# A prologue in another order: mask copies on ScalarE, GpSimd's splits and constants rearranged, set-up work moved behind a later unit

## The chip, the cores and the metric

The kernel runs as one program on one core of a Trainium2 chip. The metric is the device time in microseconds, from the start of the program to the end of its last instruction; a run is timed several times and its median is compared. The core has five engines that work beside each other, each through its own list of instructions in order: TensorE (PE in the profile, its weight loads PEld), VectorE (DVE), ScalarE (ACT), GpSimd (POOL) and SyncE (SP, which here only issues DMA transfers). They wait for each other by semaphores.

## The reference

Attention over clusters, then a mixture of experts on its output. The batch is 4, with 8 heads, 768 positions and head dimension 64.

```
q_assign = argmax(q_n . c_n), k_assign = argmax(k_n . c_n)       # 16 centroids for each head
scores   = where(q_assign == k_assign, q k^T / 8, -1e9)
attn     = softmax(scores);  out = attn v
x        = out as (3072 tokens, 512)
g_idx    = argmax(x w_group), e_idx = argmax(x w_expert[g_idx])  # 4 groups of 4 experts
y        = softmax weights of both choices * (relu(x w1) w2)     # of the chosen expert alone
```

## The kernel before

The 32 heads (4 batches of 8) are worked on in pairs: pair p holds heads 2p and 2p + 1, one in partitions 0 to 63 and one in 64 to 127. For each pair the kernel loads k, q and v (`load`, `loadv`), splits each into a 16-bit part and a 16-bit rest, the "hi" and the "lo" part (`split`, `splitv`: ScalarE writes hi; lo comes from VectorE, or in the prologue for pairs 0 and 1 partly from GpSimd), computes the clusters (`assign`: 36 small matmuls, then maxima and comparisons on VectorE that give a one-hot row), and copies the parts by DMA into the tiles `A` (hi parts and mask rows) and `B` (`spread`).

A head is then 9 coarse and 9 fine units of 512 columns. A coarse unit (`coarse`) is one product on TensorE and one maximum over it on VectorE (`tensor_reduce`, "reduce" below); after the ninth, `rowmax` turns the 9 maxima into one row for each query. A fine unit (`fine`) multiplies again with the mask and the row maximum in the contraction, ScalarE takes the exp (`p32`), GpSimd the rest of it (`pl`, the line with `op=ALU.subtract` in `fine`), and 5 units later (`LAG`) TensorE multiplies it with v (`av`, "P·V" below, 16 matmuls). Coarse units run 13 units ahead of the fine ones at first and up to 18 later. `pp` holds 7 buffers of `p32` and `pl`.

The masks of heads 0 to 3 are made by `mask_now`: six transposes for q and six for k, each followed by a copy of 16 rows into `A`, by ScalarE for q and by VectorE for k. The row maximum of heads 0 and 1 is made in `rowmax`'s first branch: a last maximum on VectorE (`m7`, 6 columns from 18), a small ScalarE copy into `st`, six transposes on TensorE, and a ScalarE copy into `A`.

The prologue, up to the loop over fine units, is written out by hand: constants (32 rows of each of the 16 halves of the eight `A` tiles, and two columns of each of the four `V` tiles, set by GpSimd), the centroids, pair 0, coarse units of head 0, the splits of pair 1 on GpSimd, four coarse units of head 1, the clusters and masks of pair 1, and the load of pair 2. Then `R.setup` and `cfg["setup"]` make what the router and the experts need later: the router's weights `WR` (two VectorE instructions after the load of `wf`), `ones`, `low`, `cb` and others, lists of slots by some fifty small GpSimd instructions, and seven DMA transfers (`wf`, `zrow`, five of `table`). In the loop `at(g, f)` runs f beside fine unit g.

A scheduler of the compiler's front end decides how the instructions of one engine stand in its list, within the dependences and within the edges that `tc.issue_after(x)` adds: whatever the block traces on x's engine stands behind x there.

Of the kernel before, what the change touches and what calls it, by code (L numbers as in the profile page):

```python
# [14 lines left out]
F32 = mybir.dt.float32  # L15
I32 = mybir.dt.int32
AF = mybir.ActivationFunctionType
ALU = mybir.AluOpType
AX = mybir.AxisListType
# [6 lines left out]
SQ = 16.0  # L26
# [10 lines left out]
def attention(ctx, tc, qT, kT, vr, cen, R, DEN, cfg):  # L37
# [16 lines left out]
    EARLY = ()  # L54
    GAP, RM, RL = 1, 2, 9
    EVEN = 16
    DVE_LO = [()] * 8
    WHOLE16 = 2, 3, 4
    DVE_END = (0, 2, 4, 6, 8), (0, 1, 2, 3, 7, 8)
# [21 lines left out]
    def load(p):  # L81
        b, pr = p // NP, p % NP
        kx = ld.tile([P, S], F32, name="kx")
        qx = ld.tile([P, S], F32, name="qx")
        nc.sync.dma_start(out=kx, in_=kT[b, pr])
        nc.sync.dma_start(out=qx, in_=qT[b, pr])
        st[p] = [qx, kx]
# [61 lines left out]
    def pairs(x):  # L149

        h = struct.pack("<e", x)
        return struct.unpack("<f", h + h)[0]

    for i in range(8):
        nc.gpsimd.memset(QA[i].bitcast(F32)[64:96], pairs(PSHIFT))
        nc.gpsimd.memset(KA[i].bitcast(F32)[64:96], pairs(SQ * SQ))
    for i in range(4):
        nc.gpsimd.memset(V[i][:, :, :, 128:130], SQ)

# [20 lines left out]
    def split(p, w, pool=False):  # L180
        x = st[p][w]
        if (p, "s") not in st:

            st[p, "s"] = sp.tile([P, 4, S], F16, name="parts")
        hi, lo = (st[p, "s"][:, i] for i in ((0, 2), (3, 1))[w])
        with bound():
            nc.scalar.activation(out=hi, in_=x, func=AF.Copy, scale=SQ)
        lo_part(lo, x, hi, pool)
        st[p, w] = (hi, lo)
# [40 lines left out]
    def splitv(p, pool=False):  # L230
        x = st[p][2]
        vt = V[p % 4]
        with bound():
            nc.scalar.activation(out=vt[:, :, :, 64:128], in_=x, func=AF.Copy, scale=SQ)
        lo_part(vt[:, :, :, 0:64], x, vt[:, :, :, 64:128], pool)
# [50 lines left out]
                nc.sync.dma_start(out=KA[h % 8][64:64 + C], in_=mk[64 + C * i:64 + C * i + C])  # L286
            ready.add(h)

    def mask_now(h, pool):

        for t, dst in ((0, QA[h]), (1, KA[h])):
            tp = pool[0].tile([P, 512], F32, name=pool[1]).bitcast(F16)
            for c in range(NCH):
                nc.tensor.transpose(out=tp[0:OZ, c * P:(c + 1) * P], in_=ozs[h // 2][:, t, h % 2, c], identity=ident)
            if t == 0:
                nc.scalar.activation(out=dst[64:64 + C], in_=tp[64:64 + C, :S], func=AF.Copy, scale=-32768.0)
            else:
                nc.vector.tensor_scalar(out=dst[64:64 + C], in0=tp[64:64 + C, :S], scalar1=-32768.0, scalar2=32768.0, op0=ALU.mult, op1=ALU.add)

# [10 lines left out]
    def coarse(h, u, pool=(ps_c, "psc")):  # L310

        assert h < 4 or h in ready
        j, i = u // 3, u % 3
        if u == 0:
            cparts[h] = MP[h % 3]
        mp = cparts[h][:, j]
        pc = pool[0].tile([P, 512], F32, name=pool[1])
        off = 0
        for (c, k0, k1) in segs(u, S):
            last["mm"] = nc.tensor.matmul(out=pc[:, off:off + k1 - k0], lhsT=QA[h % 8][0:80, c * P:(c + 1) * P], rhs=KA[h % 8][0:80, k0:k1], start=True, stop=True)  # L320
            off += k1 - k0
        n = 1 + i % 2
        nc.vector.tensor_reduce(out=(mp[:, 0, 0:1], mp[:, :, 1], mp[:, 1, 0:1])[i], in_=pc.rearrange("p (a x) -> p a x", a=n), axis=AX.X, op=ALU.max)  # L323
        if u == 8 and h > 1:
            if h < 5:
                nc.gpsimd.memset(MH[h % 3][:, NCH:P], 0.0)
            nc.vector.tensor_reduce(out=pc[:, 0:NCH], in_=cparts.pop(h).rearrange("p j a x -> p (j a) x"), axis=AX.X, op=ALU.max)
            nc.vector.tensor_scalar(out=MH[h % 3][:, 0:NCH], in0=pc[:, 0:NCH], scalar1=-1.0 / (SQ * SQ), scalar2=None, op0=ALU.mult)
# [92 lines left out]
    def at(g, f, *a):  # L421
        jobs.setdefault(int(g), []).append((f, a))
# [63 lines left out]
    banks = itertools.cycle(((ps_c, "psc"), (ps_f, "psf")))  # L486
    for u in range(9):
        coarse(0, u, next(banks))
    mask_now(1, (ps_o, "pso"))
    spread(0, (1,), part=(1,))  # L490
    run(rowmax(0))

    splitv(0, True)
    split(1, 1, True)
    split(1, 0, True)
    splitv(1, True)
    with tc.issue_after(last["mm"].ins), tc.issue_after(last["max"].ins):
        for u in range(AHEAD0 - 9):
            coarse(1, u, next(banks))
        run(assign(1))  # L500
        spread(1)
        mask_now(2, (ps_m, "psm"))
        mask_now(3, (ps_m, "psm"))
    load(2)
    loadv(2)
    at(0, split, 2, 0)
    at(1, split, 2, 1)
    R.setup()
    cfg["setup"]()
    prev = []  # L510

    def av_next(g):
# [40 lines left out]
class Router:  # L553
# [9 lines left out]
    def setup(self):  # L563
        nc, const, N, E, BS, KD = self.nc, self.const, self.N, self.E, self.BS, self.KD
        wf = const.tile([P, KD, 20], F32, name="wf")
        nc.sync.dma_start(out=wf, in_=self.wr)
        self.WR = const.tile([P, 2, KD, 20], F16, name="WR")
        nc.vector.tensor_scalar(out=self.WR[:, 0], in0=wf, scalar1=WRS, scalar2=None, op0=ALU.mult)
        nc.vector.scalar_tensor_tensor(out=self.WR[:, 1], in0=wf, scalar=WRS, in1=self.WR[:, 0], op0=ALU.mult, op1=ALU.subtract)
        self.ones = const.tile([P, P], F16, name="ones")  # L570
        nc.vector.memset(self.ones, 1.0)
        self.low = const.tile([P, P], F16, name="low")
        nc.gpsimd.affine_select(out=self.low, in_=self.ones, pattern=[[1, P]], compare_op=ALU.is_gt, fill=0.0, base=0, channel_multiplier=-1)
        self.desc = const.tile([P, 30, 4], F32, name="desc4")
        nc.gpsimd.iota(self.desc, [[0, 30], [-1, 4]], base=4, channel_multiplier=0, allow_small_or_imprecise_dtypes=True)
        self.ebase = const.tile([P, E], F32, name="ebase")
        nc.gpsimd.iota(self.ebase, [[BS, E]], base=0, channel_multiplier=0, allow_small_or_imprecise_dtypes=True)
        self.cb = const.tile([P, E], F32, name="cb")
        NT = N // P
        self.pay = const.tile([P, NT, 2], F32, name="pay")  # L580
        nc.gpsimd.iota(self.pay[:, :, 0], [[P, NT]], base=0, channel_multiplier=1, allow_small_or_imprecise_dtypes=True)
        zrow = const.tile([P, 2 * KD], F16, name="zrow")
        nc.vector.memset(zrow, 0.0)
        nc.sync.dma_start(out=self.xbuf[N:N + 1].rearrange("o (p x) -> (o p) x", p=P), in_=zrow)
        em = self.em = const.tile([P, (E + 1) * BS // P // 5, 2], F32, name="em")
        nc.vector.memset(em[:, :, 0:1], float(N))
        nc.vector.memset(em[:, :, 1:2], 0.0)
        self.lg, self.last, self.sent, self.apart, self.done = {}, {}, [], True, -1

        self.reset()  # L590
# [1123 lines left out]
```

## Time and profile before

| | us |
|---|---|
| time, median of 3 runs | 705.99 |
| lowest, highest run | 704.86, 707.33 |
| the profiled execution's own time | 705.2 |
| its span, first to last instruction | 703.4 |
| TensorE busy in the span | 676.3 (96%) |
| VectorE busy | 580.7 (83%) |
| ScalarE busy | 501.8 (71%) |
| GpSimd busy | 461.3 (66%) |

The change touches the first 60 us or so of the span. In the page's strip of 40 slices (17.6 us each) TensorE is busy five tenths in the first slice, eight in the second and third and nine or more from the fourth on. All times of rows below count from the start of the span. A busy time of TensorE is modelled and matmuls overlap, so its idle time reads as a lower bound.

### The profile page before, as it was taken

What the parts mean: (1) busy time and instruction counts of PE and PEld (TensorE: products, weight loads), DVE (VectorE), ACT (ScalarE), POOL (GpSimd) and SP (SyncE); (2) the same over time, 40 slices, a digit from 0 to 9 for tenths busy, and PEclk for the clock granted to TensorE, in tenths of its full rate; (3) what the DMA queues carried; (4) which work ended last, traced back from release to release, by engine and by line L of the source; (5) the groups of instructions that cost most, each with busy time, mean ns of one, the idle gap of its engine ahead of it and who ended that gap; (6) DMA issues with size and microseconds to landing.
All of it is one profiled execution on the core that took longest, in us unless ns stands there. A gap on an engine that the chain in (4) does not pass through costs nothing.

```text
span 703.4 us, 25950 instructions
## 1 busy us (share of the span) xinstructions
PE 676.3 (96%) x10528; PEld 582.3 (83%) x10528; DVE 580.7 (83%) x1226; ACT 501.8 (71%) x948; POOL 461.3 (66%) x522
## 2 busy tenths in 40 slices
PE   5889999999999999999999999999999999999995
PEld 3677888888878888887878867898799999999995
DVE  5998988899888998989888766868688788888861
ACT  5558898898897988878897346664655666766742
POOL 9768888899998999989995044335534254443542
PEclk9999999999999999999999999999999999999998
DMA  8865736647566375641765089889989789888711
GB/s 254 204 183 150 202 102 170 157 111 210 105 160 166 92 208 108 134 119 31 175 140 108 25 307 334 306 323 245 347 233 323 243 306 292 299 295 289 215 65 36
DMA packets 89527, 136.74 MB, mean 194 GB/s; under 512 B 41507, under 2 KB 59427, under 8 KB 89384
## 3 DMA queue, kind: packets, MB, share of 16 engines
q1 hardware_dynamic: 83884, 121.32, 61.1%
q0 software_dynamic: 5344, 13.38, 5.7%
q8 instruction: 102, 1.67, 1.0%
q14 instruction: 41, 0.34, 0.2%
q10 hardware_dynamic: 156, 0.03, 0.0%
HBM read 93.17 MB, written 13.99 MB: 152 GB/s over the span
## 4 chain that ended last, share of the span: by engine, by line
PE 71%; DVE 13%; ACT 9%; issue 4%; DMA 2%; POOL 1%; POOLq 0%; DVEq 0%; SPq 0%; ACTq 0%
PE psh L1065 17%; PE psy L1099 14%; PE pso L395 11%; PE psf L362 6%; PE psc L320 6%; PE psf L363 6%; DVE mpart L323 5%; PE psy L1123 4%; ACT p L367 3%; PE psm L1151 2%; PE psm L253 2%; ACT ph L371 1%; PE psm L1033 1%; PE psm L633 1%; ACT psm L853 1%
## 5 line engine op out<-in xcount | busy, mean ns | idle before, releaser
L374 POOL TENSOR_TENSOR pl<-p 128x512 f16<-128x512 f32 x193 | 198.6, 1055 | 19.7 <-ACT p L367 18.5
L323 DVE TENSOR_REDUCE mpart<-psc 128x1 f32<-128x512 f32 (+1 forms) x282 | 188.4, 680 | 18.4 <-PE psc L320 16.5
L367 ACT ACTIVATE p<-psf 128x512 f32<-128x512 f32 x288 | 172.0, 599 | 40.2 <-PE psf L363 37.0
L395 PE MATMUL pso<-V,pl 128*128 128x65 f16 (+1 forms) x1968 | 161.1, 193 | 0.0
L362 PE MATMUL psf<-A 82*128 82x384 f16 (+2 forms) x576 | 143.9, 275 | 2.1 <-ACT p L367 0.8
L363 PE MATMUL psf<-B 128*128 128x384 f16 (+2 forms) x576 | 143.7, 274 | 0.0
L395 PEld LDWEIGHTS <-pl 128*128 128x128 f16 x1968 | 130.8, 97 | 1.8 <-issue 0.4
L395 PEld LDWEIGHTS <-p 128*128 128x128 bf16 x1632 | 112.4, 98 | 20.4 <-issue 0.5
L395 PE MATMUL pso<-V,p 128*128 128x65 f16 x1632 | 120.8, 193 | 0.0
L374 POOL TENSOR_TENSOR pl<-p,ph 128x512 f16<-128x512 f32 x84 | 96.8, 1160 | 22.6 <-POOL pl L374 8.3
L320 PE MATMUL psc<-A 80*128 80x512 f16 (+1 forms) x376 | 107.0, 328 | 4.8 <-DVE mpart L323 3.4
L1070 ACT ACTIVATE hh<-psh 128x256 f16<-128x256 f32 (+14 forms) x136 | 45.8, 347 | 74.2 <-PE psh L1065 72.6
L1023 POOL DMA_INDIRECT xg<-xbuf,ri x32 | 37.8, 1180 | 75.5 <-PE psm L1033 30.2
L1071 DVE SCALAR_TENSOR_TENSOR hl<-psh,hh 128x256 f16<-128x256 f32 (+14 forms) x136 | 47.0, 366 | 33.0 <-ACT hh L1070 32.3
L363 PEld LDWEIGHTS <-B 128*128 128x128 f16 x576 | 56.8, 99 | 13.1 <-issue 4.0
L1065 PE MATMUL psh<-xT,wh0a 128*128 128x272 f16 (+14 forms) x512 | 65.9, 246 | 1.7 <-DMA st<-w 1.0
L362 PEld LDWEIGHTS <-A 82*128 82x128 f16 x576 | 56.0, 98 | 10.2 <-issue 1.5
L1065 PE MATMUL psh<-xT,wl0a 128*128 128x272 f16 (+7 forms) x256 | 59.4, 245 | 0.0
L1065 PE MATMUL psh<-xT,wh0b 128*128 128x272 f16 (+6 forms) x448 | 57.1, 245 | 0.1
L371 ACT CAST ph<-p 128x512 f16<-128x512 f32 x84 | 51.9, 618 | 2.3
L1065 PE MATMUL psh<-xT,wl0b 128*128 128x240 f16 (+6 forms) x224 | 52.3, 244 | 0.0
L320 PEld LDWEIGHTS <-A 80*128 80x128 f16 x384 | 37.4, 99 | 15.9 <-issue 6.3
(330 smaller groups left out, 1600.6 us busy)
## 6 DMA issues: line engine op xcount, KB each, us to landing
st<-w SPq DMA_DIRECT2D x88, 512.0 KB
B<-parts SPq DMA_DIRECT2D x64, 192.0 KB
wh<-w SPq DMA_DIRECT2D x21, 512.0 KB
wl<-w SPq DMA_DIRECT2D x19, 512.0 KB
kx<-kT SPq DMA_DIRECT2D x16, 384.0 KB
qx<-qT SPq DMA_DIRECT2D x16, 384.0 KB
vx<-vr SPq DMA_DIRECT2D x16, 384.0 KB
A<-parts SPq DMA_DIRECT2D x32, 192.0 KB
```

The source lines that it names most:

```text
L320: last["mm"] = nc.tensor.matmul(out=pc[:, off:off + k1 - k0], lhsT=QA[h % 8][0:80, c * P:(c + 1) * P], rhs=KA[h % 8][0:80, k0:k1], start=T ...
L323: nc.vector.tensor_reduce(out=(mp[:, 0, 0:1], mp[:, :, 1], mp[:, 1, 0:1])[i], in_=pc.rearrange("p (a x) -> p a x", a=n), axis=AX.X, op=ALU ...
L362: nc.tensor.matmul(out=o, lhsT=KA[h % 8][0:82, ks], rhs=QA[h % 8][0:82, q0:q1], start=True, stop=False)
L363: nc.tensor.matmul(out=o, lhsT=KBs[h][:, ks], rhs=QBs[h][:, q0:q1], start=False, stop=True)
L367: cfg["exp"] = nc.scalar.activation(out=p32, in_=pf, func=AF.Exp, scale=QK / (SQ * SQ))
L371: nc.scalar.copy(out=ph, in_=p32)
L374: lo = (nc.vector if u in (EARLY if h < 2 else DVE_LO[h % 8] if h < NH - 2 else DVE_END[h - NH]) else nc.gpsimd).tensor_tensor(out=pl, in0 ...
L395: nc.tensor.matmul(out=O[:, col:col + v.shape[-1]], lhsT=p[:, bs], rhs=v, start=c == 0 and q == 0 and i == 0, stop=c == NCH - 1 and i == l ...
L1065: self.mm = nc.tensor.matmul(out=ph[:, 0:n], lhsT=w[:, k, f * P:(f + 1) * P], rhs=xT[:, a, k, 0:n], start=i == 0, stop=i == 3 * KD - 1)
L1070: nc.scalar.activation(out=hh[:, f], in_=ph[:, 0:M], func=AF.Relu)
L1071: self.ev = nc.vector.scalar_tensor_tensor(out=hl[:, f], in0=ph[:, 0:M], scalar=0.0, in1=hh[:, f], op0=ALU.max, op1=ALU.subtract)
L1099: self.mm = nc.tensor.matmul(out=py[:, 0:n], lhsT=w[:, f, d * P:(d + 1) * P], rhs=a[:, f, 0:n], start=i == 0, stop=i == len(prods) - 1)
```

## The change

Six edits, all in `attention`:

- `mask_now(1, ...)` gets `both=True`: the mask copy of k for head 1 is a ScalarE activation, with scale and bias from `mscale` and `mbias`, where a VectorE `tensor_scalar` stood.
- GpSimd sets the constants of `A` tiles 0 and 1 only at the start; those of tiles 2 to 7 come behind the splits of pair 1.
- The splits of pair 1 come in the order k, q, v of pair 0, v of pair 1, where v of pair 0 came first.
- `load(2)` is written ahead of the coarse units of head 1 and of the clusters and masks of pair 1.
- The splits of pair 2 get an edge behind the maximum that `rowmax` made last on VectorE when they run (`last["max"]`, head 0's).
- `R.setup` and `cfg["setup"]` run beside fine unit 6 (`SETUP = 6`), behind the latest reduce on VectorE and the latest `pl` on GpSimd, where they stood ahead of the loop.

```diff
--- before.py
+++ after.py
@@ -54,6 +54,7 @@
     EARLY = ()
     GAP, RM, RL = 1, 2, 9
     EVEN = 16
+    SETUP = 6
     DVE_LO = [()] * 8
     WHOLE16 = 2, 3, 4
     DVE_END = (0, 2, 4, 6, 8), (0, 1, 2, 3, 7, 8)
@@ -151,9 +152,12 @@
         h = struct.pack("<e", x)
         return struct.unpack("<f", h + h)[0]
 
-    for i in range(8):
-        nc.gpsimd.memset(QA[i].bitcast(F32)[64:96], pairs(PSHIFT))
-        nc.gpsimd.memset(KA[i].bitcast(F32)[64:96], pairs(SQ * SQ))
+    def constants(heads):
+        for i in heads:
+            nc.gpsimd.memset(QA[i].bitcast(F32)[64:96], pairs(PSHIFT))
+            nc.gpsimd.memset(KA[i].bitcast(F32)[64:96], pairs(SQ * SQ))
+
+    constants(range(2))
     for i in range(4):
         nc.gpsimd.memset(V[i][:, :, :, 128:130], SQ)
 
@@ -286,7 +290,7 @@
                 nc.sync.dma_start(out=KA[h % 8][64:64 + C], in_=mk[64 + C * i:64 + C * i + C])
             ready.add(h)
 
-    def mask_now(h, pool):
+    def mask_now(h, pool, both=False):
 
         for t, dst in ((0, QA[h]), (1, KA[h])):
             tp = pool[0].tile([P, 512], F32, name=pool[1]).bitcast(F16)
@@ -294,6 +298,8 @@
                 nc.tensor.transpose(out=tp[0:OZ, c * P:(c + 1) * P], in_=ozs[h // 2][:, t, h % 2, c], identity=ident)
             if t == 0:
                 nc.scalar.activation(out=dst[64:64 + C], in_=tp[64:64 + C, :S], func=AF.Copy, scale=-32768.0)
+            elif both:
+                nc.scalar.activation(out=dst[64:64 + C], in_=tp[64:64 + C, :S], func=AF.Identity, scale=mscale[64:64 + C], bias=mbias[64:64 + C])
             else:
                 nc.vector.tensor_scalar(out=dst[64:64 + C], in0=tp[64:64 + C, :S], scalar1=-32768.0, scalar2=32768.0, op0=ALU.mult, op1=ALU.add)
 
@@ -320,7 +326,7 @@
             last["mm"] = nc.tensor.matmul(out=pc[:, off:off + k1 - k0], lhsT=QA[h % 8][0:80, c * P:(c + 1) * P], rhs=KA[h % 8][0:80, k0:k1], start=True, stop=True)
             off += k1 - k0
         n = 1 + i % 2
-        nc.vector.tensor_reduce(out=(mp[:, 0, 0:1], mp[:, :, 1], mp[:, 1, 0:1])[i], in_=pc.rearrange("p (a x) -> p a x", a=n), axis=AX.X, op=ALU.max)
+        last["red"] = nc.vector.tensor_reduce(out=(mp[:, 0, 0:1], mp[:, :, 1], mp[:, 1, 0:1])[i], in_=pc.rearrange("p (a x) -> p a x", a=n), axis=AX.X, op=ALU.max)
         if u == 8 and h > 1:
             if h < 5:
                 nc.gpsimd.memset(MH[h % 3][:, NCH:P], 0.0)
@@ -486,14 +492,16 @@
     banks = itertools.cycle(((ps_c, "psc"), (ps_f, "psf")))
     for u in range(9):
         coarse(0, u, next(banks))
-    mask_now(1, (ps_o, "pso"))
+    mask_now(1, (ps_o, "pso"), True)
     spread(0, (1,), part=(1,))
     run(rowmax(0))
 
-    splitv(0, True)
     split(1, 1, True)
     split(1, 0, True)
+    splitv(0, True)
     splitv(1, True)
+    load(2)
+    constants(range(2, 8))
     with tc.issue_after(last["mm"].ins), tc.issue_after(last["max"].ins):
         for u in range(AHEAD0 - 9):
             coarse(1, u, next(banks))
@@ -501,12 +509,20 @@
         spread(1)
         mask_now(2, (ps_m, "psm"))
         mask_now(3, (ps_m, "psm"))
-    load(2)
     loadv(2)
-    at(0, split, 2, 0)
-    at(1, split, 2, 1)
-    R.setup()
-    cfg["setup"]()
+
+    def behind_max(w):
+        with tc.issue_after(last["max"].ins):
+            split(2, w)
+
+    at(0, behind_max, 0)
+    at(1, behind_max, 1)
+    def setup():
+        with tc.issue_after(last["red"].ins), tc.issue_after(cfg["lo"].ins):
+            R.setup()
+            cfg["setup"]()
+
+    at(SETUP, setup)
     prev = []
 
     def av_next(g):
```

What the edits do to the lists of three engines is shown next. The line numbers of the changed program are higher than those of the kernel before, by 4 in `mask_now`, by 6 in `coarse`, `rowmax` and `fine`, and by 16 in the router and the experts; `p_...` are exps by buffer, `A_165` to `A_168` the A tiles of heads 0 to 3.

VectorE around the last maximum of head 1 (`m_742` before, `m_656` after); `mpart_200` are reduces of head 2. Before:

```order
L323 TENSOR_REDUCE mpart_200<-psc 128x2
L260 TENSOR_TENSOR psm<-psm,mx 128x384
L334 TENSOR_REDUCE m_742<-mpart_199 128x6
L323 TENSOR_REDUCE mpart_200<-psc 128x1
L261 TENSOR_TENSOR psm<-psm,desc 128x384
L199 SCALAR_TENSOR_TENSOR parts<-kx,parts 128x768
L263 TENSOR_REDUCE mw<-psm 128x24
L323 TENSOR_REDUCE mpart_200<-psc 128x1
L265 TENSOR_TENSOR oh<-psm,mw 128x6x32 x2
```

In the changed program:

```order
L340 TENSOR_REDUCE m_656<-mpart_199 128x6
L329 TENSOR_REDUCE mpart_200<-psc 128x1
L265 TENSOR_TENSOR psm<-psm,desc 128x384
L203 SCALAR_TENSOR_TENSOR parts<-kx,parts 128x768
L267 TENSOR_REDUCE mw<-psm 128x24
L584 TENSOR_SCALAR WR<-wf 128x80
L269 TENSOR_TENSOR oh<-psm,mw 128x6x32 x2
L585 SCALAR_TENSOR_TENSOR WR<-wf,WR 128x80
L587 MEMSET ones 128x128
L599 MEMSET zrow 128x4
L602 MEMSET em 128x85
L603 MEMSET em 128x85
```

`WR`, the memsets and, one row further down, `cb` now stand behind the maximum of head 1 and ahead of the fourth reduce of head 2; before, `WR` and `cb` stood ahead of that maximum and the memsets at the very start.

ScalarE from the exp of fine unit 3 to that of unit 6; `parts<-kx` and `parts<-qx` are hi parts of a pair, `A_167` and `A_168` the mask copies of q for heads 2 and 3, `st<-m_...` the copy of head 1's maximum. Before:

```order
L367 ACTIVATE p_632<-psf 128x512
L367 ACTIVATE p_691<-psf 128x512
L296 ACTIVATE A_167<-psm 16x768
L367 ACTIVATE p_717<-psf 128x512
L296 ACTIVATE A_168<-psm 16x768
L187 ACTIVATE parts<-kx 128x768
L187 ACTIVATE parts<-qx 128x768
L234 ACTIVATE V_176<-vx 128x12x64
L335 ACTIVATE st<-m_742 128x6
L339 ACTIVATE A_166<-psf,obias,oscale 18x768
L367 ACTIVATE p_758<-psf 128x512
```

In the changed program:

```order
L373 ACTIVATE p_546<-psf 128x512
L373 ACTIVATE p_605<-psf 128x512
L238 ACTIVATE V_175<-vx 128x12x64
L373 ACTIVATE p_631<-psf 128x512
L191 ACTIVATE parts<-kx 128x768
L300 ACTIVATE A_167<-psm 16x768
L191 ACTIVATE parts<-qx 128x768
L300 ACTIVATE A_168<-psm 16x768
L238 ACTIVATE V_176<-vx 128x12x64
L341 ACTIVATE st<-m_656 128x6
L345 ACTIVATE A_166<-psf,obias,oscale 18x768
L373 ACTIVATE p_672<-psf 128x512
```

The hi parts of k and q of pair 3 stood behind both mask copies and now stand ahead of the first and the second; all six first exps now stand ahead of the mask copies.

GpSimd around the set-up; `pl<-p_584` before is the pl of fine unit 0, `pl<-p_672` and `pl<-p_788` after are those of units 6 and 7. Before:

```order
L197 TENSOR_TENSOR V_174<-vx,V_174 128x12x64
L573 AFFINE_SELECT low<-ones 128x128
L575 IOTA desc_502 128x120
L577 IOTA ebase 128x16
L581 IOTA pay 128x24
L785 IOTA io 128x16
L792 MEMSET capr 1x1 x13
L792 MEMSET capr 1x2
L792 MEMSET capr 1x1
L796 MEMSET capn 1x1 x16
L799 MEMSET four 1x1 x16
L803 IOTA io_573 128x288
```

In the changed program:

```order
L380 TENSOR_TENSOR pl<-p_672 128x512
L591 IOTA desc_706 128x120
L593 IOTA ebase 128x16
L597 IOTA pay 128x24
L801 IOTA io 128x16
L808 MEMSET capr 1x1 x13
L808 MEMSET capr 1x2
L808 MEMSET capr 1x1
L812 MEMSET capn 1x1 x16
L815 MEMSET four 1x1 x16
L819 IOTA io_777 128x288
L821 MEMSET svals 128x36
```

The block from the iota of `desc` to the memset of `svals` stood behind the split of v, ahead of all pl; it now stands behind the pl of unit 6, and the pl of unit 7 follows it. `low` and two iotas come behind that one.

## Rows read from the trace of the kernel before

**Rows 1.** Stretches of the span: length, busy us of each engine, granted clock, DMA

```profile
20.60:23.90 3.30, 1.90 (x17) 1.08 (x15) 3.21 (x7) 1.21 (x2) 3.30 (x56) 0.98 0.89 231
23.90:27.10 3.20, 3.20 (x16) 1.83 (x14) 2.80 (x7) 1.72 (x3) 1.70 (x7) 0.50 1.05 270
...
34.00:38.40 4.40, 3.16 (x56) 2.13 (x55) 4.40 (x9) 1.90 (x3) 0.00 (x0) 1.00 0.92 205
...
44.00:54.00 10.00, 10.00 (x188) 8.07 (x187) 9.77 (x21) 5.63 (x10) 9.93 (x9) 1.00 0.61 181
...
64.00:110.00 46.00, 45.58 (x866) 37.39 (x863) 41.09 (x91) 40.57 (x79) 39.74 (x38) 1.00 0.60 154
```

**Rows 2.** TensorE's waits from 38 to 110 us: total, times, longest

```profile
PE psf L338 <- ACT st L335: 0.4, 1, 0.4
```

**Rows 3.** Timeline of VectorE, 20 to 46 us: start, us, instruction, idle before

```profile
21.01 0.56 DVE L298 TENSOR_SCALAR A<-pso 16x768 f16<-16x768 f16 x1
21.59 0.17 DVE L334 TENSOR_REDUCE m<-mpart 128x6 f32<-128x18 f32 x1
...
25.57 0.16 DVE L594 COPY cb<-ebase 128x16 f32<-128x16 f32 x1
...
28.28 0.57 DVE L568 TENSOR_SCALAR WR<-wf 128x80 f16<-128x80 f32 x1
...
29.30 0.58 DVE L569 SCALAR_TENSOR_TENSOR WR<-wf,WR 128x80 f16<-128x80 f32 x1
...
31.10 1.50 DVE L199 SCALAR_TENSOR_TENSOR parts<-kx,parts 128x768 f16<-128x768 f32 x1
...
38.00 0.16 DVE L334 TENSOR_REDUCE m<-mpart 128x6 f32<-128x18 f32 x1
...
44.63 0.99 DVE L199 SCALAR_TENSOR_TENSOR V<-vx,V 128x768 f16<-128x768 f32 x1
```

**Rows 4.** Part 5 of the page, the reduces: busy us, mean ns, idle before

```profile
L323 DVE TENSOR_REDUCE mpart<-psc 128x1 f32<-128x512 f32 (+1 forms) x282 | 188.4, 680 | 18.4 <-PE psc L320 16.5
```

**Rows 5.** Timeline of ScalarE, 18 to 33 us

```profile
18.87 0.84 ACT L187 ACTIVATE parts<-kx 128x768 f16<-128x768 f32 x1 [1.01 <-DMA kx<-kT]
...
25.97 0.84 ACT L187 ACTIVATE parts<-qx 128x768 f16<-128x768 f32 x1
...
30.18 0.80 ACT L296 ACTIVATE A<-psm 16x768 f16<-16x768 f16 x1 [0.69 <-PE psm L294]
...
31.63 0.80 ACT L296 ACTIVATE A<-psm 16x768 f16<-16x768 f16 x1
```

**Rows 6.** Timeline of TensorE, first matmul of pair 2's clusters

```profile
32.48 0.18 PE L253 MATMUL psm<-CH,parts 128*128 128x32 f16 x1 [0.23 <-ACT A L296]
```

**Rows 7.** Chain that ended last, matmuls of pair 0's clusters: start, us, count

```profile
8.57 1.11 PE psf L253 x35
```

**Rows 8.** Timeline of GpSimd, 21 to 52 us, single instructions

```profile
21.01 0.29 POOL L573 TENSOR_SCALAR_AFFINE_SELECT low<-ones 128x128 f16<-128x128 f16 x1
21.27 0.38 POOL L575 IOTA desc<- 128x120 f32 x1
...
23.82 0.12 POOL L805 MEMSET svals<- 128x36 bf16 x1
...
24.14 0.15 POOL L807 IOTA svals<- 128x6 bf16 x1
...
40.78 1.04 POOL L374 TENSOR_TENSOR pl<-p 128x512 f16<-128x512 f32 x1 [7.28 <-ACT p L367]
...
44.77 1.76 POOL L374 TENSOR_TENSOR pl<-p 128x512 f16<-128x512 f32 x1
...
50.20 1.03 POOL L374 TENSOR_TENSOR pl<-p 128x512 f16<-128x512 f32 x1
```

**Rows 9.** Timeline of TensorE, first P·V of fine units 10 and 14

```profile
48.17 0.19 PE L395 MATMUL pso<-V,p 128*128 128x65 f16 x1
...
52.75 0.22 PE L395 MATMUL pso<-V,p 128*128 128x65 f16 x2
```

## The prediction

> **What bounds the kernel now.** I read the stretches of the span first. Behind 64 us TensorE is busy 45.58 of 46 us, and it stays so; from 44 to 54 us it is busy all the time [rows 1]. A change in the prologue can therefore give back only what TensorE loses before about 40 us: 1.40 of the 3.30 us from 20.6 to 23.9, 1.24 of the 4.40 from 34 to 38.4, and the stretch from 23.9 to 27.1, where the granted clock was 0.50 (the 1.2 GHz level) [rows 1]. Second view, TensorE's waits: from 38 us on it waits 0.4 us for ScalarE's copy that starts the row maximum of head 1 [rows 2]. That one ends a longer starvation. TensorE takes its list in order, and the six transposes of that row maximum stand ahead of every fine unit from unit 6 on. They wait for VectorE's last maximum of head 1, at 38.00 [rows 3]. So the first question is how much sooner than 38.00 that maximum comes. After it TensorE is full, and the second question is what the change puts in its way there. Third view, the engines' own lists, for both questions.
>
> **Part 1: what leaves VectorE and ScalarE's turn before 38.00.** VectorE loses the mask copy of k, head 1 (0.56 at 21.01), the copy of cb (0.16) and two WR instructions (0.57, 0.58): 1.87 us by their rows [rows 3]. In addition the lo part of k, pair two, took 1.50 there where a like one takes 0.99 (44.63) [rows 3]: if it is alone next time, 0.5 more. Upper bound of the gain: 2.4 us.
> But VectorE is not alone in that chain. The order shows that ScalarE now makes the copies of k and q of pair three ahead of the mask copy of q, head 3, where both stood behind it. Before, that copy ended at 31.63 + 0.80 = 32.43 [rows 5], and the next assignment's 36 matmuls started right behind it, at 32.48, waiting for it [rows 6]. After: minus 0.58, since the maximum of head 0 comes at once behind the ninth reduce (21.59 against 21.01 [rows 3]); plus 0.84, since two copies of 0.84 come in front of it and one, q of pair two, leaves (25.97) [rows 5]; minus at most 0.69, ScalarE's wait ahead of 30.18 that may be filled [rows 5]. It ends between 32.0 and 32.7. Behind it come the assignment (1.11 for 35 matmuls [rows 7]), one coarse unit with its hand-over (about 0.6, an estimate from the reduce of 0.68 [rows 4]) and four VectorE instructions, two reduces of 0.68 and two of about 0.57: 4.2 us, against 5.57 from 32.43 to 38.00. The maximum then comes at 36.2 to 36.9, 1.1 to 1.8 sooner. Lower bound 0.7: in TensorE's new list the P·V of units 2 and 3 stands ahead of the masks of head 3 and waits for GpSimd's pl, one of which took 1.76 where others take 1.03 [rows 8]. I take **1.4 us sooner**, ScalarE's path, not VectorE's sum.
>
> **Part 2: what is put behind it.** The router's and the experts' setup moves behind fine unit 6. On GpSimd it ran from 21.01 to 24.14 + 0.15 = 24.29, less about 0.15 for one memset of another part: 3.1 us [rows 8], when GpSimd had nothing urgent. Now 2.67 of it (21.27 to 23.94) stand between the pl of unit 6 and that of unit 7, the rest one unit later. GpSimd is idle 7.28 us ahead of unit 6 [rows 8], but the setup stands behind unit 6, so that idle time does not take it. From 44 to 54 GpSimd is busy 9.93 of 10 us [rows 1]; its pl queue is dense and P·V in TensorE's list waits for it. How late may pl be? For unit 10 it ends at 44.77 + 1.76 = 46.53 and P·V starts at 48.17; for unit 14 at 51.23 against 52.75 [rows 8, 9]. The slack is 1.64 and 1.52. A queue 3.1 later eats it and holds TensorE 3.1 - 1.52 = **1.6 us**. Bounds: zero, if TensorE is late there for another reason; 2.2, below.
> VectorE gets the two WR and cb (1.31 by their rows [rows 3]) and four small memsets behind the maximum of head 1, ahead of the fourth reduce of head 2. TensorE's order puts the coarse unit that needs that reduce's bank behind more fine units and the first P·V, so it costs 0 to 0.3, and what it costs is inside the 1.6, because the pl queue does not wait for it.
>
> **Parts that cost nothing.** The mask copy of k, head 1, on ScalarE (0.80 like its like at 30.18) falls into ScalarE's idle time: it waited 1.01 for kx at 18.87 [rows 5] and then for the maximum. The two copies of pair two behind it must end before that maximum, at 21.0; their loads are issued ahead of two spreads now. If kx or qx came 1 us late, the chain would start 1 us late; that cover is thin and is in the lower bound. GpSimd's q and k first: the lo parts come sooner, but TensorE's assignment of pair one stands behind coarse unit 8 as before, so nothing starts sooner. Constants of later units: they fill the place of the setup ahead of the first pl. SP: the seven setup transfers move in among the spreads of pairs two and three; what they hold up are spreads for heads 6 and 7 and the loads of pair four, which nobody waits for there.
>
> **A rule against the change.** The pl of unit 10 took 1.76 instead of 1.03 beside VectorE's lo part of v, 44.63 to 45.62 [rows 3, 8]. The Trainium skill, "SBUF — State Buffer", section "SBUF: two separate sides", says that such a VectorE instruction with two SBUF operands and a GpSimd instruction that reads SBUF lock each other out for a whole instruction. The row agrees in kind: 0.73 was lost, not the whole 0.99.
> As a mechanism here: the second such lo part hits unit 12 now; with GpSimd 3.1 later it can hit unit 10 or one before, where the slack is 1.64 with only one hit in it. Then TensorE is held 3.1 + 0.73 - 1.64 = 2.2 us.
>
> **Sum.** -1.4 + 1.6 = +0.2. The profiled execution took 705.2 (span 703.4), so 705.4 by its own time; the median of the three runs, 705.99, lies 0.8 above it: 706.2. A difference of 0.3% (2.1 us) is about what can be told from none here, so this forecast is no measurable change.
>
> **Rivals.**
> Both hits early: 2.2 - 1.4 = +0.8, time 706.8. For it: the hit of 0.73 is in the trace. Against: if TensorE is held, VectorE's reduces come later too, and the second lo part with them. Chance 0.15, still within 0.3%.
> Faster: VectorE's full 2.4 arrive, because ScalarE's 0.69 and more are filled, and the pl queue holds TensorE only 0.2. In addition the granted clock may not fall at 23.9, as TensorE idles less ahead of it: the 3.2 us at half speed are worth 1.6 of TensorE's time, of which perhaps half shortens the way to the exps. That gives -2.2 to -3.0: 703.0 to 703.8. For it: VectorE is busy without a pause up to 38.4 (4.40 of 4.40 [rows 1]). Against: the new place of two ScalarE copies. Chance 0.22.
> Slower: TensorE, starved for pl at units 7 to 14, is given the lower clock again. Before, the clock fell after a stretch with 1.40 us of idle time in 3.30 [rows 1]; a hold of 2.2 us within units 8 to 10 would be like it. Price: 3.2 us at half speed, 1.6 us, all on the path as TensorE is full there. +0.8 + 1.6 = +2.4, time 708.4. It decides from the point where the hold for pl is as long as the idle time that stood ahead of the fall, 1.40. Against: 1.24 us of idle time from 34 to 38.4 left the clock at 1.00 [rows 1]. Chance 0.12.
>
> **How the numbers follow.** The forecast has 0.51; with the early hits, 0.66 lie within 0.3%, 0.22 are faster, 0.12 slower by more. The range runs from the faster case to the slower one, 703.5 to 708.2: it leaves out the far half of each, together under 2 in 10. It holds the bounds -2.2 to +1.5 around 706.0 with the spread of the runs (704.86 to 707.33).
>
> **What would show it.** In the profile after: the maximum of head 1 (VectorE, six columns from 18) at 36.2 to 36.9 for 38.00; the mask copies of heads 2 and 3 on ScalarE near 31 and 32.5; GpSimd without a pause from the pl of unit 6 to some unit behind 14, with 2.7 us of iotas and memsets in it; waits of TensorE's weight loads for GpSimd's pl near 42 to 50 us, 1 to 2 us in all, where there are none now; the granted clock's low stretch somewhere near 24. The forecast is wrong if no wait for pl shows (then the gain of part 1 stays), if the maximum of head 1 comes at 38 or later, or if a second stretch at 0.50 shows up.

## The result and the profile after

The changed kernel is slower: 714.09 us (median of 6 runs, 712.13 to 716.74) against 705.25 for the kernel before in the same runs; ratio 1.0119, 95% interval 1.0098 to 1.0139. The forecast was 706.2 with a range up to 708.2. The profiled execution took 716.08, its span is 714.1. In the new file the lines called L320 to L338 in the rows of before stand 6 further down, lo of k, q and v at L203 (was L199), the mask copy at L304, pl at L380.

First the stretches of the span, with the columns of [rows 1].

```profile
44.00:54.00 10.00, 5.63 (x84) 4.20 (x84) 9.77 (x7) 3.42 (x6) 10.00 (x53) 0.93 0.61 170
54.00:64.00 10.00, 7.81 (x130) 6.40 (x130) 8.33 (x18) 3.29 (x6) 3.31 (x4) 0.73 0.15 47
64.00:110.00 46.00, 44.74 (x814) 35.99 (x811) 41.41 (x91) 38.41 (x74) 37.69 (x36) 1.00 0.62 158
```

TensorE, busy 10.00 of 10 us from 44 to 54 before, is busy 5.63. VectorE is "busy" 9.77 with 7 instructions where it had 21. Behind 64 us TensorE is nearly as full as in [rows 1], 44.74 of 46; the loss lies ahead. The timeline of VectorE shows which one it is:

```profile
33.20 0.56 DVE L304 TENSOR_SCALAR A<-psm 16x768 f16<-16x768 f16 x1 [3.06 <-PE psm L298]
...
39.30 0.16 DVE L340 TENSOR_REDUCE m<-mpart 128x6 f32<-128x18 f32 x1
...
47.32 7.70 DVE L203 SCALAR_TENSOR_TENSOR V<-vx,V 128x768 f16<-128x768 f32 x1
54.94 0.55 DVE L265 TENSOR_TENSOR psm<-psm,desc 128x384 f32<-128x384 f32 x1
...
56.47 0.94 DVE L203 SCALAR_TENSOR_TENSOR V<-vx,V 128x768 f16<-128x768 f32 x1
```

The lo part of v, pair two, took 7.70 us; in [rows 3] it took 0.99, and its like at 56.47 takes 0.94. So it stood still for 6.76 us, and behind it, in VectorE's list, stood the reduces. Beside it, GpSimd's timeline:

```profile
42.08 1.04 POOL L380 TENSOR_TENSOR pl<-p 128x512 f16<-128x512 f32 x1 [9.05 <-ACT p L373]
...
44.74 0.60 POOL L815 MEMSET four<- 1x1 f32 x16
45.30 0.36 POOL L819 IOTA io<- 128x288 f16 x1
45.62 0.12 POOL L821 MEMSET svals<- 128x36 bf16 x1
45.71 1.03 POOL L380 TENSOR_TENSOR pl<-p 128x512 f16<-128x512 f32 x1
...
47.19 7.01 POOL L380 TENSOR_TENSOR pl<-p 128x512 f16<-128x512 f32 x7
58.02 1.04 POOL L380 TENSOR_TENSOR pl<-p 128x512 f16<-128x512 f32 x1 [3.83 <-ACT p L373]
```

Seven pl run without a gap from 47.19 to 54.20; VectorE's instruction ends at 55.02, 0.82 us after the last one, which is about its own running time. It got nothing until GpSimd had nothing left. TensorE's waits from 38 to 66 us (total, times, longest) name the consequence, and its timeline shows where the wait ends:

```profile
PE psc L326 <- DVE mpart L329: 7.0, 3, 6.1
...
PE pso L401 <- POOL pl L380: 0.4, 2, 0.2
```
```profile
56.13 0.58 PE L326 MATMUL psc<-A 80*128 80x512 f16 x1 [6.11 <-DVE mpart L329]
...
57.05 0.32 PE L401 MATMUL pso<-V,p 128*128 128x65 f16 x2
...
62.19 0.19 PE L401 MATMUL pso<-V,p 128*128 128x65 f16 x1
```

P·V of unit 10 starts at 57.05 instead of 48.17 and that of unit 14 at 62.19 instead of 52.75 [rows 9]: 8.9 and 9.4 us, of 10.7 between the two spans. Within the standstill, TensorE being idle since 50.0, the granted clock falls to 0.50 (1.2 GHz), from 52.5 to 59.4, and at 86.84 us TensorE waits 0.86 for a transfer, as it did not before. The chain that ended last holds the same piece: "47.41 7.61 DVE V L203".

### The profile page after: what moved, and what is told of

It is laid out like the page before. It is cut to its first block, busy times and chain, and to the rows that moved or that the text cites. A ratio compares the mean times of both kernels' runs of the same rounds, so it can differ in the third digit from the quotient of the medians.

```text
span 714.1 us, 25970 instructions
## 1 busy us (share of the span) xinstructions
PE 681.2 (95%) x10528; PEld 585.1 (82%) x10528; DVE 586.7 (82%) x1225; ACT 502.5 (70%) x949; POOL 459.6 (64%) x522
## 4 chain that ended last, share of the span: by engine, by line
PE 61%; DVE 16%; ACT 9%; issue 4%; DMA 4%; POOL 3%; SPq 1%; POOLq 0%; ACTq 0%; DVEq 0%
PE psh L1081 17%; PE psy L1115 14%; PE pso L401 8%; DVE mpart L329 6%; PE psf L368 4%; PE psc L326 4%; PE psf L369 4%; PE psy L1139 3%; ACT p L373 3%; PE psm L1167 2%; PE psm L257 1%; DMA kx<-kT 1%; DVE V L203 1%; PE psm L1049 1%; ACT ph L377 1%
## 5 line engine op out<-in xcount | busy, mean ns | idle before, releaser
L380 POOL TENSOR_TENSOR pl<-p 128x512 f16<-128x512 f32 x193 | 196.5, 1041 | 31.1 <-ACT p L373 29.8
L369 PE MATMUL psf<-B 128*128 128x384 f16 (+2 forms) x576 | 145.4, 277 | 0.0
L401 PE MATMUL pso<-V,p 128*128 128x65 f16 x1632 | 122.4, 194 | 0.0
L380 POOL TENSOR_TENSOR pl<-p,ph 128x512 f16<-128x512 f32 x84 | 96.7, 1160 | 22.1 <-POOL pl L380 7.7
L1081 PE MATMUL psh<-xT,wl0a 128*128 128x272 f16 (+7 forms) x256 | 59.4, 245 | 0.0
```

The costliest lines, as they stand in the source:

```text
L369: nc.tensor.matmul(out=o, lhsT=KBs[h][:, ks], rhs=QBs[h][:, q0:q1], start=False, stop=True)
L380: lo = (nc.vector if u in (EARLY if h < 2 else DVE_LO[h % 8] if h < NH - 2 else DVE_END[h - NH]) else nc.gpsimd).tensor_tensor(out=pl, in0 ...
L401: nc.tensor.matmul(out=O[:, col:col + v.shape[-1]], lhsT=p[:, bs], rhs=v, start=c == 0 and q == 0 and i == 0, stop=c == NCH - 1 and i == l ...
L1081: self.mm = nc.tensor.matmul(out=ph[:, 0:n], lhsT=w[:, k, f * P:(f + 1) * P], rhs=xT[:, a, k, 0:n], start=i == 0, stop=i == 3 * KD - 1)
```

## The experiments

Times are medians beside runs of the kernel before on the same chip; before itself took 705.7 to 706.7 in most groups of runs, but 713.97 beside e9 to e11 and 713.24 beside e18, so there only ratios say anything.

**e1, e7: take VectorE's two-SBUF instruction away** (the lo part of v, both of whose inputs lie in SBUF).

```
-        elif now[0] < EVEN:
+        elif now[0] < 9:
```


> Kernel after, but the lo part of v of pairs two and three goes the way that later pairs take (ScalarE through PSUM halves), so VectorE has no instruction with two SBUF operands there. Theory L (lock): the loss is VectorE's lo of v, which took 7.70 us instead of 0.99 beside seven pl back to back on GpSimd, because it could not start until GpSimd's queue had a gap. Then 714.1 - 6.7 = about 707.4, range 706.0 to 709.0, and no VectorE instruction over 2 us between 44 and 56. Theory C (chain and clock): TensorE at 1.2 GHz from 8.2 to 32.1 us, and again from 52.5 to 59.4, makes the loss: within 1.5 of 714.1. Theory H (hold, the prediction's part 2): P.V waits for pl that are 3.1 us late: within 1.5 of 714.1, since GpSimd's queue is as it was.

> Kernel before with the lo parts of v, pairs two and three, by ScalarE through PSUM, as in run e1. Theory L: there was little conflict to take away before (two pl longer by 0.7 each), so 704.5 to 706.5, and the whole difference of 8.8 between after and e1 is the starvation. Theory G (the PSUM way is a gain by itself of several us, and starvation is only part): 700 to 703.

On after (e1) 705.32 against 706.00 (ratio 0.9997, 0.9979 to 1.0015): the whole loss is gone, a little more than theory L had said, and theories C and H fall. On before (e7) 706.25 against 705.69 (1.0005, 0.9986 to 1.0024): no gain by itself. GpSimd's queue in e1 is as late as in after, and TensorE waits for it 1.0 us:

```profile
PE pso L401 <- POOL pl L380: 1.0, 3, 0.5
```

**e2, e3, e4: which part of the change.** e2 puts the setup back ahead of the loop, e3 moves the setup alone, e4 has `SETUP = 5`.

> Kernel after with the router's and experts' setup back where it stood before the loop; the rest of the change stays. Theory L: GpSimd's backlog behind unit 6 goes, so the lo of v takes 1 to 1.8 us again; what stays is the later maximum of head 1 (39.30 against 38.00): 705.3 + 1.3 = 706.6, range 705 to 708.5. Theory C: the long stretch at 1.2 GHz has its cause in the prologue's new order and stays: 711 to 715. Theory H: only the hold goes, 1.6 us: about 712.5.

> Kernel before with the setup alone moved behind unit 6. Theory L: the lo of v meets the same backlog of pl and starves: 705.3 + 6 to 8 = 711 to 713.5. If it meets GpSimd inside the setup instead, whose instructions are short and read little from SBUF, it is not starved, and the time is 705 to 707; the trace tells which. Theory C: 704 to 706. Theory H: 705.3 + 1.6 = 706.9.

> Kernel after with the setup behind unit 5 instead of unit 6, so that GpSimd does it in the 9.05 us in which it waits for unit 6's exp. Theory L: no backlog of GpSimd at the lo of v: it takes 1 to 1.8 us, and the time is 705.5 to 708. VectorE's part of the setup may now delay the maximum of head 1 by up to 1.3 us, which is in that range. Theory C: 712 to 715. Theory H: the hold goes, 1.6 us: about 712.5.

e3: 715.15 against 706.00, ratio 1.0122 (1.0096 to 1.0148). The moved setup alone makes the loss, which is above the range of theory L, and its lo part of v took 7.70 us as well:

```profile
38.11 0.16 DVE L335 TENSOR_REDUCE m<-mpart 128x6 f32<-128x18 f32 x1
...
46.13 7.70 DVE L200 SCALAR_TENSOR_TENSOR V<-vx,V 128x768 f16<-128x768 f32 x1
```

In e2 the starvation is gone, with lo parts of v of 0.95 and 1.26. It was still slower than theory L said, 710.05 (1.0059, 1.0039 to 1.0079), and its trace shows another reason: with the constants of later units ahead of the setup, ebase comes late, and the copy of cb holds VectorE ahead of the maximum of head 0; that of head 1 comes at 42.72.

```profile
24.29 0.20 DVE L606 COPY cb<-ebase 128x16 f32<-128x16 f32 x1 [3.32 <-POOL ebase L589]
24.38 0.16 DVE L340 TENSOR_REDUCE m<-mpart 128x6 f32<-128x18 f32 x1
```

e4: 707.88 (1.0025, 1.0003 to 1.0048), no starvation, lo parts 1.75 and 1.09; but WR and the memsets now stand ahead of the maximum of head 1 (38.64), for which TensorE waits 2.5 us. With e1's edit added (e8) it was no better:

> Kernel after with both mends: the setup behind unit 5, in GpSimd's idle time, and the lo parts of v, pairs two and three, through PSUM. Theory L: neither starvation nor backlog; what is left of the change is its prologue. If the prologue gives what the prediction's part 1 said (1.4 us), 704.0 to 705.0; if the maximum of head 1 is no earlier than 38.00 (e4: 38.64), 705.5 to 707.5. Theory C: over 707, with a spread that follows the granted clock of the first 32 us.

706.69 (1.0018, 1.0000 to 1.0035), maximum at 38.60.

**e5, e6: gaps in GpSimd's stream.** e5 is after with `nc.gpsimd.memset(wz.bitcast(F32), 0.0)` behind the pl of units 8 to 14; e6 is before with ten of them behind unit 6.

> Kernel after with seven memsets of GpSimd (0.27 us each, of a tile that nothing reads any more) put singly between the pl of units 8 to 15. Theory L1: VectorE's lo of v is kept out only by instructions of GpSimd that read SBUF through the shared port, back to back; a memset reads nothing, so VectorE gets in at the first one: the lo part takes at most 2 us and the time is 706 to 709, though GpSimd has 1.9 us more to do. Theory L2: what keeps VectorE out is that GpSimd's next instruction is always ready, whatever it is: the lo part starves 7.7 us or longer, and the time is 714 to 717.

> Kernel before with ten memsets of GpSimd (0.27 us each) behind unit 6, one to three of them between any two pl; setup and prologue as before. GpSimd is later by 2.7 us as in kernel after, but its stream is broken by memsets. L1: no long starvation, the lo parts take 1 to 2 us; P.V may wait for pl for up to 1 us: 705.5 to 707.5. L2: one lo part takes over 5 us: 710 to 714. Theory H (the prediction's hold): 706.9.

e5: 708.91 (1.0032, 1.0012 to 1.0052), although GpSimd had 1.9 us more to do; in its profile TensorE waits 2.4 us for pl. e6: 707.06 (1.0019, 0.9999 to 1.0039), lo parts 1.24 and 1.51. In e5 VectorE asks 0.14 after a pl has begun (46.41) and gets in at the memset; the next pl waits for it:

```profile
46.27 1.03 POOL L380 TENSOR_TENSOR pl<-p 128x512 f16<-128x512 f32 x1
47.25 0.30 POOL L529 MEMSET wz<- 128x256 f32 x1
47.52 1.50 POOL L380 TENSOR_TENSOR pl<-p 128x512 f16<-128x512 f32 x1
```
```profile
46.41 1.72 DVE L203 SCALAR_TENSOR_TENSOR V<-vx,V 128x768 f16<-128x768 f32 x1
```

So a memset on GpSimd opens the way, as theory L1 has it. But back-to-back pl alone don't close it: in [rows 3, 8] the lo part at 44.63 got in within a dense row of pl, one of which took 1.76 for it. What was different in after?

**e9, e10: the moment of the request.** e9 puts `nc.vector.memset(lo[:, 0, 0:3], 0.0)` ahead of the lo part, which then comes one instruction later; e10 makes ones and low ahead of the loop.

> Kernel after, GpSimd's stream unchanged, but VectorE's lo of v comes one instruction later (behind the multiplication by desc and a short memset of a part of its own output, about 0.7 us in all). In after the request came 0.13 us into the first of seven pl; here about 0.8 into it. Theory P (the moment of the request in the current pl decides; in the traces so far every request 0.34 or more into a pl got in behind that pl, also between back-to-back pl, and the two at 0.13 with pl behind them did not): the lo part takes at most 1.6 us, the time is 706 to 709. Theory B (GpSimd's backlog decides: its next pl had been ready for over 3 us, against 0.8 to 1.5 in before): starved again, 6 to 7.7 us, time 713 to 716.

> Kernel after with the two instructions for ones and low (VectorE 0.17, GpSimd 0.28) made ahead of the loop: the row of pl starts about 0.28 sooner and the lo of v asks about 0.3 to 0.4 into the first pl, with the backlog nearly as in after (at least 3 us). Theory P: it gets in behind the first pl, takes at most 2 us, and the time is 706 to 709. Theory B: starved, 7 us, 713 to 716.

e9: ratio 1.0145 (1.0109 to 1.0182); e10: 1.0077 (1.0051 to 1.0102), lo part 6.77, but its request fell 0.06 into a pl, not at the place aimed at. In e9 the request comes 0.73 us into the pl that begins at 43.87, and VectorE stands for eight pl. Theory P falls.

```profile
35.98 0.16 DVE L343 TENSOR_REDUCE m<-mpart 128x6 f32<-128x18 f32 x1
...
44.60 8.09 DVE L206 SCALAR_TENSOR_TENSOR V<-vx,V 128x768 f16<-128x768 f32 x1
```
```profile
43.87 8.01 POOL L383 TENSOR_TENSOR pl<-p 128x512 f16<-128x512 f32 x8
```

**e11: the mask copy** of k, head 1, back on VectorE, in e1's kernel.

> Run e1's kernel with the mask copy of k, head 1, back on VectorE. If that copy's place costs and gives nothing, 704.5 to 706.5 as e1, and the maximum of head 1 moves by less than 0.5 us; if VectorE sets that maximum (the prediction's upper bound of part 1), it comes 0.5 to 0.6 later and the time is about 0.5 more, which the timing can hardly tell. A low clock ahead of 30 us moves the maximum by more than that: with 1.00 in all of the stretch it should come at 37 to 38, with 0.50 at about 39.2.

Ratio 0.9989 (0.9973 to 1.0006), maximum of head 1 at 37.50. That copy's place can't be told by the time; what the traces show of it comes below.

**e12, e13, e14: how late GpSimd is.** e12 has `SETUP = 20`; e13 makes capn and four ahead of the loop, e14 capr as well.

> Kernel after with the setup behind unit 20 instead of unit 6: the lo parts of v (units 9 to 14) meet GpSimd without the setup's backlog, and behind unit 16 no two-SBUF lo parts are left on VectorE there. All else as in after, and VectorE's share of the setup is out of the way of the maximum of head 1. Theory L: no starvation; against before a ratio of 0.996 to 1.001: the prologue's gain (up to 2.0 us, the maximum of head 1 at 36 in executions with the clock at 1.00 ahead of 30 us; none in the others), less up to 1 us for the 3.1 us that GpSimd now does among later pl. If something else in the change costs several us: ratio over 1.005.

> Kernel after with 1.2 of the setup's 3.1 us on GpSimd (the memsets of capn and four) ahead of the loop: when the lo of v asks, the next pl will have been ready for about 2.7 us instead of 3.7. In run e10, with 2.6, it starved 6.77 us; in before, with 1.46, it got in behind the current pl. Theory B (backlog): starved again, lo part 5 to 7 us, ratio to before 1.006 to 1.012.

> Kernel after with 1.75 of the setup's 3.1 us on GpSimd (capr, capn and four) ahead of the loop: the next pl ready for about 2.1 us at the request. Between 1.46 (got in) and 2.6 (starved) nothing has been seen yet. If the point lies above 2.1: lo part under 2 us and ratio 0.998 to 1.003; if below: starved for 4 to 6 us, ratio 1.005 to 1.01.

e12: 705.50 against 706.74 (0.9985, 0.9960 to 1.0009): without the starvation nothing is lost. e13: 713.81 (1.0094, 1.0065 to 1.0123), lo part 6.61. e14: 708.17 (1.0027, 1.0006 to 1.0049), and it overthrew theory B too. VectorE's timeline:

```profile
26.00 6.34 DVE L203 SCALAR_TENSOR_TENSOR parts<-qx,parts 128x768 f16<-128x768 f32 x1
...
49.69 1.13 DVE L203 SCALAR_TENSOR_TENSOR V<-vx,V 128x768 f16<-128x768 f32 x1
```

At 49.69, with the next pl's exp done 2.3 us before that pl, it got in. At 26.00 another lo part (q, pair one) starved beside the first six pl, whose exps were done only 0.3 to 0.8 us before them. There the tiny memsets now stand directly ahead of the first pl. And the pl themselves differ. A view of pl by its tile (duration in ns: min, median, max; first and last start), for e14 from 25 to 32 us, then from 46 to 56:

```profile
L380 POOL TENSOR_TENSOR pl<-p x6: 1028/1029/1031, 25.5 to 30.5; 128x512 f16<-128x512 f32 x6
```
```profile
L380 POOL TENSOR_TENSOR pl<-p x8: 1036/1042/1757, 46.5 to 55.4; 128x512 f16<-128x512 f32 x8
```

The same view of before and of after, 40 to 54 and 43 to 55 (after's one of 1040 is not in the dense row, it is unit 6's, which waited for its exp):

```profile
L374 POOL TENSOR_TENSOR pl<-p x12: 1033/1041/1760, 40.8 to 53.3; 128x512 f16<-128x512 f32 x12
```
```profile
L380 POOL TENSOR_TENSOR pl<-p x9: 1028/1029/1040, 42.1 to 53.2; 128x512 f16<-128x512 f32 x9
```

In every stretch where VectorE starved the pl take 1.03 us with hardly any spread; where it got in they take 1.032 to 1.05, or up to 1.85 where they waited for VectorE. By the timelines each such stretch of 1.03 begins behind a burst of memsets of one element with no wait for an exp between.

**e15 to e18: the burst by itself.** e15 adds to before, behind unit 6, and nothing else (e18: 32 of them):

```
+            for r in range(16):
+                nc.gpsimd.memset(tiny[:, r:r + 1], float(2 ** r))
```

e16 is after with the tiny memsets behind unit 5 and five iotas in their place behind unit 6; e17 is e16 without the iotas.

> Kernel before with 16 memsets of one element (0.60 us in all, GpSimd) behind the pl of unit 6, nothing else changed. Theory M: it is such a burst of tiny instructions with no wait behind it that makes GpSimd run its following instructions without a gap (pl of 1.030 us in place of 1.040), and in that mode VectorE's two-SBUF instruction does not get in until GpSimd's queue runs dry: pl of 1.03, one lo part of v takes over 5 us, ratio 1.006 to 1.012. Theory B (GpSimd's lateness): only 0.6 us late: lo parts of 1 to 1.8 us, ratio 0.998 to 1.002.

> Kernel after, but the 47 tiny memsets (capr, capn, four: 1.75 us) stand behind unit 5, with GpSimd's wait for unit 6's exp behind them, and five iotas of 288 columns (0.36 us each) take their place behind unit 6: GpSimd is as late as in after (3.1 us), the next pl ready for over 3 us when the lo of v asks. Theory M: pl of 1.04, the lo parts take under 2 us, ratio 0.998 to 1.003. Theory B: starved as in after, 6 to 8 us, ratio 1.009 to 1.013.

> Kernel after with only the 47 tiny memsets moved behind unit 5, into GpSimd's idle time; the rest of the setup stays behind unit 6. Theory M: no starvation; with the prologue's gain (the maximum of head 1 up to 2 us sooner where the clock is at 1.00 ahead of 30 us) and a queue only 1.35 us later: ratio 0.995 to 1.001, about as e12. Theory B: 1.35 us later than before, ready for about 2 us: no starvation either, the same range, so this run is for the size, not for the choice.

> Run e15 with 32 tiny memsets (1.2 us) in place of 16, so that the exp of the next units is done before GpSimd comes to them in nearly every execution. Theory M: pl of 1.03 behind the burst in the profile itself, one lo part of v over 5 us, and all timed runs near 714 (ratio 1.008 to 1.013), where e15's fell in two groups, 708 to 709 and 714 to 717. Theory B: 1.2 us late, as e17, whose lo parts took 1.1 and 1.3 us: ratio 0.999 to 1.003.

e15: 714.01 against 706.15 (1.0108, 1.0069 to 1.0146), in two groups: 708.05 and 709.00; 714.01, 714.52 and 717.00. The profile is the one of 709.00, and shows the way out: behind one pl of 1.03 GpSimd had to wait for an exp, its pl were of 1.04 from then on, and the lo parts took 1.24 and 1.26. That VectorE starved in the three slow executions is not shown, as none was profiled.

```profile
42.98 0.59 POOL L515 MEMSET tiny<- 1x1 f32 x16
43.54 1.03 POOL L374 TENSOR_TENSOR pl<-p 128x512 f16<-128x512 f32 x1
44.82 1.04 POOL L374 TENSOR_TENSOR pl<-p 128x512 f16<-128x512 f32 x1 [0.25 <-ACT p L367]
```

e18, where that wait doesn't come: ratio 1.0102 (1.0071 to 1.0133), all seven runs from 720.18 to 724.63 against 713.24, and in the profile

```profile
42.60 1.11 POOL L515 MEMSET tiny<- 1x1 f32 x32
43.68 8.01 POOL L374 TENSOR_TENSOR pl<-p 128x512 f16<-128x512 f32 x8
```
```profile
45.48 7.03 DVE L199 SCALAR_TENSOR_TENSOR V<-vx,V 128x768 f16<-128x768 f32 x1
```

GpSimd's next pl had been ready there for only 1.2 to 1.5 us. e16, with the next pl ready for 3.9 us (3.75 in after), but without the burst: 707.65 (1.0025, 1.0006 to 1.0044), and in its profile, from 42 to 54 us:

```profile
L380 POOL TENSOR_TENSOR pl<-p x10: 1034/1041/1762, 42.9 to 53.5; 128x512 f16<-128x512 f32 x10
```
```profile
36.16 0.16 DVE L340 TENSOR_REDUCE m<-mpart 128x6 f32<-128x18 f32 x1
...
45.16 1.81 DVE L203 SCALAR_TENSOR_TENSOR V<-vx,V 128x768 f16<-128x768 f32 x1
```

Theory M holds against theory B in e16 and e18; e15's times fit it, and e17 was not made to choose. e17, the version that theory M suggests: 706.63 (0.9994, 0.9976 to 1.0012). It and e12 are the best of the study, and neither can be told from before.

## Why the prediction was wrong

**What bounds the kernel** was read rightly: TensorE is full behind 44 us, and what it loses there stays lost. The question put second, what the change puts in its way there, was the one that decided.

**The step that failed is the rule against the change.** The prediction had the place (a lo part of v beside a dense row of pl) and took the price from one row: 0.73 us, paid by a pl [rows 8]. It then made that a rival of +0.8. What the runs showed is the other side: VectorE paid, 6.76 us, through the reduces behind it. Where the next pl's start is not preceded by a burst the price is what the prediction said (e16: the lo part of 1.81 waits for one pl, then the next pl takes 1.76). The rule as cited from the Trainium skill, "SBUF — State Buffer", section "SBUF: two separate sides", has the pair held for a whole instruction by whichever starts first. For one instruction the traces agree; in e18 VectorE's stood from 45.48 through the rest of one pl and six more, and the measurement decides. Before's trace could not price that: its setup too has the burst (21 to 24 us), but GpSimd waits for an exp ahead of its first pl. It did show that a late VectorE would hold TensorE: of its waits from 38 to 110 us the largest, which the prediction passes over beside the 0.4 of [rows 2], is for the reduces.

```profile
PE psc L320 <- DVE mpart L323: 1.1, 2, 0.8
```

Two of the prediction's own signs of being wrong came: the maximum of head 1 behind 38, and a second stretch at 0.50.

**Part 2, the hold for pl**, forecast at 1.6 us, was 0.4 in after and 1.0 in e1, where no starvation covers it; in e16, with GpSimd as late, TensorE doesn't wait for pl at all but 1.9 us for reduces. The term was of the right kind and too large. VectorE's setup behind the maximum cost nothing that shows (e12, e17).

**Part 1, the maximum of head 1** at 36.2 to 36.9 instead of 38.00, failed in the profile of after (39.30) and was met or passed in others. It goes with the granted clock, which differs ahead of 32 us between profiled executions whose order is the same up to there. After had 0.50 from 8.2 to 32.1; e1 (39.21), e10 (39.38) and e17 (39.77) had it until about 32. With 1.00 from 24 us on it came at 35.98 (e9), 36.32 (e12), 36.27 (e13), 36.16 (e16). The same stretch in after and in e9:

```profile
27.10:34.00 6.90, 6.88 (x87) 5.44 (x86) 3.81 (x8) 5.07 (x9) 5.35 (x5) 0.64 0.52 122
```
```profile
27.10:34.00 6.90, 6.03 (x134) 5.22 (x133) 6.28 (x11) 6.13 (x9) 5.14 (x5) 1.00 0.65 153
```

In after TensorE is busy all the time at the lower clock and does 87 instructions in place of 134; VectorE, the busier of the two in e9, waits for its mask transposes (3.06 at 33.20). How much of this the new order gives is not shown, since no profile has the old order at 1.00 from 24 to 30 us. At like clocks the orders lie close: with 0.50 from about 8 to 28 or 29 us the old one had 38.11 to 38.69 (e3, e6, e7) and the new one 38.38 (e5); with 0.50 from about 24 to 27 the old one had 38.00 (before; 39.22 and 38.84 where it lasted to about 30, e15 and e18) and the new one, but for the mask copy, 37.50 (e11). The prediction had taken the clock of before's one execution for that of all. Even the 1.7 to 2.0 us of the good executions don't stand out in e12's interval.

**The clock's rival** (TensorE starved, the clock falls again) happened, but as a consequence: 6.11 us of idle time, with 0.50 from 52.5 to 59.4. The cause that it named, the hold for pl, was not long enough.

**The parts that cost nothing**: the time can't tell the mask copy's place (e11), but the traces can. In the four profiles with the copy on VectorE and the clock at 1.00 until 23 us (before, e11, e15, e18) TensorE waits 1.0 or 1.1 us for it at about 22, and the clock falls to 0.50 at about 24. With the copy on ScalarE and 1.00 until 23 that wait is gone, and the clock stays at 1.00 past 27 in e4, e8, e9, e13 and e14; in e2, where cb holds VectorE, it falls. The stretches of e11, then of e13, whose maxima of head 1 came at 37.50 and 36.27:

```profile
20.60:23.90 3.30, 1.89 (x25) 1.18 (x22) 3.21 (x7) 1.17 (x2) 3.24 (x11) 1.00 1.02 290
23.90:27.10 3.20, 3.20 (x14) 1.78 (x14) 2.82 (x6) 1.19 (x3) 1.14 (x4) 0.51 0.92 315
```
```profile
20.60:23.90 3.30, 3.19 (x17) 1.66 (x15) 2.89 (x7) 1.25 (x3) 3.25 (x22) 1.00 1.04 289
23.90:27.10 3.20, 2.50 (x25) 1.73 (x24) 3.20 (x7) 1.70 (x4) 2.95 (x26) 1.00 0.90 296
```

The prediction had a clock that stays up in its case "faster", but not as the copy's doing. The constants of later units cost nothing only because the setup moves away behind them (e2).

## What to carry to other kernels

Where VectorE has an instruction with two SBUF operands beside a dense row of GpSimd instructions that read SBUF, don't price the conflict by one overlap: ask whether anything makes GpSimd pause (a wait, a memset), and what stands behind VectorE's instruction. Keep bursts of tiny GpSimd instructions away from such a row, or put them where a wait follows. And a conflict that is harmless in one order of the same instructions says nothing of another.

## What the runs showed of the hardware that was not expected

Behind 15 or more GpSimd memsets of one element each (15 in e13, one of them of two elements, 16 in e15, 32 in e18), and until GpSimd next waited for an exp (e15) or VectorE got in at a memset (e5), its tensor instructions of 128x512 took 1.028 to 1.032 us instead of 1.032 to 1.05, and VectorE's two-SBUF instruction did not get in between them for 6 to 8 instructions; without two-SBUF instructions the same mode cost nothing (e1: pl of 1.03, ratio 0.9997). Memsets of 128x256, one to three at a time (e6), and twelve instructions in a row, mostly iotas (e16), did not bring it about. Why the burst does it, how few suffice, and whether the shortness of its instructions or their number counts, stays open.
